# Soft mixture of experts after pooled attention, on one core: value scale from ScalarE's sums of magnitudes, the first batch's low value parts on GpSimd, and matmuls of ones in TensorE's empty stretches of the first blocks

## The chip, the core and the metric

The kernel runs on one core of one Trainium2 chip. The metric is the time of one execution in device microseconds. The engines are TensorE (PE in the profile; its weight loads are PEld), VectorE (DVE), ScalarE (ACT), GpSimd (POOL) and SyncE (SP, which issues DMAs). Each works through its own queue in order, and they meet by semaphores.

## What is computed

Keys and values are pooled 4 by 4, multiplied by a weight, and used both as keys and as values of attention; its output feeds a soft mixture of experts. Sizes: batch 4, 12288 queries per batch, 768 keys, 128 channels; 8 experts of 4 slots each.

```python
kv_pool = kv.reshape(B, H // r, r, W // r, r, C).mean(axis=(2, 4))
kv_flat = kv_pool.reshape(B, -1, C) @ w_sr
k = v = kv_flat
s = scale * (q @ k.transpose(0, 2, 1))
a = np.exp(s - s.max(-1, keepdims=True))
a /= a.sum(-1, keepdims=True) + 1e-09
x = (a @ v).reshape(B * N, C)
logits = x @ phi
d = np.exp(logits - logits.max(0, keepdims=True))
d /= d.sum(0, keepdims=True) + 1e-09
slot_input = (d.T @ x).reshape(E, S_per_e, D)
# each expert: relu(slot_input[e] @ w1[e]) @ w2[e] -> slot_out
c = np.exp(logits - logits.max(1, keepdims=True))
c /= c.sum(1, keepdims=True) + 1e-09
out = c @ slot_out
```

## The kernel before, in words

The queries are cut into 96 blocks of 512 (24 per batch). For a block TensorE computes scores of all 768 keys, in six tiles of 128 keys by 512 queries, two tiles to a PSUM buffer (`s0`, `s1`, `s2`). For accuracy q and k are split into a high and a low part, so a tile is three matmuls (lines 494 to 496), and a block 18. VectorE takes the row maximum: three transposing reductions (501) as the buffers fill, a reduction and a product with a mask (511, 513), one small matmul on TensorE (521), a reduction (526) and a transpose (531); then four subtractions (539), which also free the score buffers. ScalarE takes two exponentials of each half (546: the half-precision high part `phi`; 550: the full one), and GpSimd subtracts the two (555), which gives the low part `plo`. TensorE then multiplies these probabilities with the values, again in high and low parts (572, 573, 580). The next block's scores want the score buffers that the subtractions free.

Values stand beside their products with phi (`v`, 160 columns: 128 channels and 32 slots), and are scaled so that half-precision parts hold them. The scale is a power of two for each of the two column groups. `kv_m` takes the largest magnitude per partition on VectorE (399, joined in 404). `kv_d` spreads it on a diagonal on ScalarE (408), `kv_s_mm` multiplies it with a matrix of ones on TensorE (412), and `kv_s_g` takes the maximum over the row, cuts it to its exponent, and gives scale and inverse (419 to 425). `kv_t_hi` and `kv_t_lo` make the high and low half-precision parts `vhi` and `vlo`: for the first batch ScalarE scales and rounds in one step (445), and VectorE makes the low part (458); for the later batches ScalarE scales in place and rounds (442, 443), and GpSimd subtracts (454).

The first batch is loaded in pieces of key halves (512 and 256 keys) that VectorE adds up as they land (330, 332) to `pooled` (334). A matmul gives the half's keys (365), ScalarE rounds them to `khi` (369), VectorE makes `klo` (374), and 386 with 389 gives the values. Later batches are added up by DMA and take the same steps while the batch before them still computes.

The program's order is not written by hand. `Plan.op` takes each piece of work with its engine, a cost, what it depends on, a priority, a time `at` from which it may stand, and PSUM buffers that it takes (`acq`) or uses. `emit` walks through an imagined time and always takes the piece that can start first, among those within 0.12 us the lowest priority number; `hot` pieces are held to be urgent, and a piece with `fill` is taken, until the imagined time given, only where it ends before any other could start. What results is a fixed order per engine; at run time only semaphores decide when each starts.

Of the kernel before, what the change touches and what calls it, by code (L numbers as in the profile page):

```python
# [186 lines left out]
def attention_then_soft_moe(ctx: ExitStack, tc: tile.TileContext, qT, kv0, kvT, w_sr, w_srT, phi, w1, w2, outT):  # L187
# [203 lines left out]
    def kv_m(b, k, h):  # L391
        if k == 0 and h == 0:
            AM[b] = (
                bp.tile([P, 2, 2], F32, tag="am", name=f"am_{b}", bufs=1),
                bp.tile([P, 2, P], BF16, tag="dg", name=f"dg_{b}", bufs=1),
                bp.tile([P, 2], F32, tag="am2", name=f"am2_{b}", bufs=1),
            )
# [1 line left out]
        nc.vector.tensor_reduce(
            out=am[:, k, h : h + 1], in_=VU[b][:, 3 * h : 3 * h + 3, VSRC[k]], axis=XY, op=ALU.max,  # L400
            apply_absolute_value=True,
        )
# [12 lines left out]

    def kv_s_g(b):
        pa = PK_.pop(b)
        pg = pa[:, 2 * P : 2 * P + 2]
        nc.vector.tensor_reduce(out=pg, in_=pa[:, : 2 * P].rearrange("p (k n) -> p k n", k=2), axis=X, op=ALU.max)
# [10 lines left out]
    def kv_t_hi(b, k):  # L430
# [10 lines left out]
        if b:  # L441
            nc.scalar.activation(v[:, :, src], v[:, :, src], AF.Copy, scale=inv[:, k : k + 1])
            nc.scalar.activation(part, v[:, :, src], AF.Copy)
        else:
            nc.scalar.activation(part, v[:, :, src], AF.Copy, scale=inv[:, k : k + 1])
# [846 lines left out]
```

## Time and profile before

| | |
|---|---|
| time, median of 3 runs | 1093.59 us (1092.59 to 1095.2) |
| time of the profiled execution | 1093.54 us |
| its span, first to last instruction | 1091.8 us |
| mean granted clock of TensorE | 0.973 |
| busy: TensorE | 1026.5 us (94%), 10098 matmuls |
| busy: VectorE | 988.0 us (90%) |
| busy: GpSimd | 870.9 us (80%) |
| busy: ScalarE | 823.3 us (75%) |
| DMA | 89.15 MB, mean 82 GB/s |

A page of the profile gives busy shares over the span, groups of instructions with their mean time, and the chain of work that ended last. A row of the timeline reads: start, duration, engine, line, operation, output and inputs; in square brackets the idle time ahead of it and what ended it. Rows of TensorE overlap, since matmuls are pipelined and their ends are modelled: the start of one to the start of the next is what a matmul costs in a full stretch. A row of windows gives, for a stretch of time, the busy time of PE, PEld, DVE, ACT and POOL, then the granted clock of TensorE, the DMA share and GB/s.

### The profile page before, as it was taken

How to read it: one execution, taken by the hardware profiler on the slowest of the kernel's cores; microseconds unless marked ns; L12 is line 12 of the kernel's file. 1: busy time of each engine (PE TensorE's matmuls, PEld its weight loads, DVE VectorE, ACT ScalarE, POOL GpSimd, SP SyncE). 2: the span in 40 equal slices, each digit the busy share in tenths (PEclk: the TensorE clock that was granted, in tenths of full speed). 3: DMA queues.
4: the chain of work that ended last, by engine and by line, in shares of the span. 5: the costliest groups of instructions: out<-in, count | busy, mean ns of one | idle time of the engine just before them, and what ended most of it. 6: DMA issues, size and time to landing. Idle time of an engine off the chain costs nothing.

```text
span 1091.8 us, 24577 instructions
## 1 busy us (share of the span) xinstructions
PE 1026.5 (94%) x10098; PEld 883.1 (81%) x10098; DVE 988.0 (90%) x1583; ACT 823.3 (75%) x1029; POOL 870.9 (80%) x503
## 2 busy tenths in 40 slices
PE   3699999999999999999999999999999999997876
PEld 2488888888888888888888888988888888886443
DVE  7899999999899999999999999999999999997895
ACT  1677778779778878878878788788788777875564
POOL 0578998888989998889999988889888898883340
PEclk9699999999999999999999999999999999999885
DMA  9306501111126401120136310120110110113398
GB/s 344 124 12 148 123 16 40 41 59 40 40 43 143 97 16 40 40 64 35 40 69 146 83 40 1 40 98 2 40 40 2 40 41 2 40 40 118 143 413 368
DMA packets 17408, 89.15 MB, mean 82 GB/s; under 512 B 1680, under 2 KB 3984, under 8 KB 11152
## 3 DMA queue, kind: packets, MB, share of 16 engines
q1 hardware_dynamic: 13408, 69.47, 17.6%
q0 software_dynamic: 3312, 17.70, 8.5%
q8 instruction: 80, 1.31, 0.5%
q10 hardware_dynamic: 576, 0.41, 0.1%
q14 instruction: 32, 0.26, 0.1%
HBM read 58.87 MB, written 25.17 MB: 77 GB/s over the span
## 4 chain that ended last, share of the span: by engine, by line
PE 84%; DVE 7%; ACT 6%; issue 2%; DMA 0%; POOL 0%; SPq 0%; DVEq 0%; ACTq 0%
PE m L572 14%; PE m L580 14%; PE m L573 13%; PE s L494 12%; PE s L496 11%; PE s L495 11%; PE m L732 2%; ACT phi L546 2%; ACT t L550 2%; PE po L1177 2%; DVE o L1186 2%; PE m L521 1%; DVE pool L332 1%; DVE t L539 1%; DVE r L501 1%
## 5 line engine op out<-in xcount | busy, mean ns | idle before, releaser
L555 POOL TENSOR_TENSOR plo<-t,phi 128x1536 f16<-128x1536 f32 x190 | 596.0, 3143 | 116.2 <-ACT t L550 102.1
L546 ACT ACTIVATE phi<-t,lnk 128x1536 f16<-128x1536 f32 x192 | 301.1, 1570 | 141.7 <-DVE t L539 141.7
L501 DVE TRANSPOSE_TENSOR_REDUCE r<-s 128x32 f32<-128x1024 f32 x288 | 355.6, 1238 | 12.2 <-PE s L496 4.6
L572 PE MATMUL m<-vhi,phi 128*128 128x161 f16 x2280 | 356.3, 234 | 8.7 <-DVE m L526 5.4
L573 PE MATMUL m<-vlo,phi 128*128 128x160 f16 x2280 | 355.5, 233 | 0.0
L539 DVE TENSOR_TENSOR t<-s,mb 128x1024 f32<-128x1024 f32 (+1 forms) x384 | 341.1, 949 | 6.9
L550 ACT ACTIVATE t<-t,lnk 128x1536 f32<-128x1536 f32 x192 | 300.9, 1568 | 0.9
L494 PE MATMUL s<-qhi,khi 128*128 128x512 f32 x576 | 240.5, 418 | 6.6 <-DVE t L539 6.6
L572 PEld LDWEIGHTS <-phi 128*128 128x128 f16 x2304 | 223.9, 98 | 23.3 <-issue 23.3
L573 PEld LDWEIGHTS <-phi 128*128 128x128 f16 x2304 | 225.2, 98 | 10.8 <-issue 10.6
L496 PE MATMUL s<-qhi,klo 128*128 128x512 f32 x576 | 227.5, 395 | 0.0
L580 PE MATMUL m<-vhi,plo 128*128 128x161 f16 x2280 | 227.1, 234 | 0.0
L495 PE MATMUL s<-qlo,khi 128*128 128x512 f32 x576 | 226.9, 394 | 0.0
L580 PEld LDWEIGHTS <-plo 128*128 128x128 f16 x2304 | 173.0, 98 | 0.6 <-issue 0.6
L484 POOL TENSOR_TENSOR qlo<-q,qhi 128x512 fp32r<-128x512 f32 x96 | 126.5, 1318 | 27.1 <-ACT qhi L480 27.1
L494 PEld LDWEIGHTS s<-qhi,khi 128*128 128x128 f32 x576 | 109.8, 191 | 27.0 <-issue 4.0
L496 PEld LDWEIGHTS s<-qhi,klo 128*128 128x128 f32 x576 | 109.3, 190 | 24.6 <-DVE klo L374 0.4
L495 PEld LDWEIGHTS s<-qlo,khi 128*128 128x128 f32 x576 | 110.2, 191 | 19.7 <-issue 0.7
L590 ACT ACTIVATE xl<-m 128x322 f32<-128x322 f32 x189 | 80.9, 428 | 43.9 <-PE m L580 42.6
L531 DVE STREAM_TRANSPOSE mb<-m 128x512 f32<-128x512 f32 x96 | 68.3, 711 | 3.3
L480 ACT ACTIVATE qhi<-q 128x512 fp32r<-128x512 f32 x96 | 59.2, 618 | 2.2 <-issue 1.3
L526 DVE TENSOR_REDUCE m<-m 128x16 f32<-128x64 f32 x96 | 21.5, 224 | 36.5 <-PE m L521 36.5
(146 smaller groups left out, 836.8 us busy)
## 6 DMA issues: line engine op xcount, KB each, us to landing
q<-qT SPq DMA_DIRECT2D x23, 1024.0 KB, 5.0
outT<-o SPq DMA_DIRECT2D x21, 1024.0 KB, 5.8
kva<-kvT POOLq DMA_DIRECT2D x9, 1536.0 KB, 11.3
kva<-kvT SPq DMA_DIRECT2D x3, 1536.0 KB, 9.9
kv<-kv SPq DMA_DIRECT2D x8, 512.0 KB, 5.7
w<-w SPq DMA_DIRECT2D x2, 1536.0 KB, 7.6
w<-w SPq DMA_DIRECT2D x4, 768.0 KB, 4.2
outT<-o SPq DMA_DIRECT2D x6, 512.0 KB, 4.1
```

The costliest lines, as they stand in the source:

```text
L484: nc.gpsimd.tensor_tensor(out=lo, in0=q_src(i), in1=hi.bitcast(F32), op=ALU.subtract)
L494: nc.tensor.matmul(s, khi[:, ks], hi, start=True, stop=False)
L495: nc.tensor.matmul(s, khi[:, ks], lo, start=False, stop=False)
L496: nc.tensor.matmul(s, klo[:, ks], hi, start=False, stop=True)
L501: nc.vector.tensor_reduce(out=MX[i][:, 2 * u : 2 * u + 2, :].rearrange("p t b -> p (t b)"), in_=S[i, u].rearrange("p t (b j) -> p (t b) j" ...
L539: nc.vector.tensor_tensor(out=TT_[i, h][:, o : o + n, :], in0=S[i, t // 2][:, u : u + n, :], in1=MX[i].unsqueeze(1).broadcast_to([P, n, BQ ...
L546: nc.scalar.activation(hi, TT_[i, h], AF.Exp, bias=lnk, scale=SCALE)
L550: nc.scalar.activation(t, t, AF.Exp, bias=lnk, scale=SCALE)
L555: eng.tensor_tensor(out=lo, in0=TT_.pop((i, h)), in1=PP[i, h], op=ALU.subtract)
L572: nc.tensor.matmul(px, p, vhi[:, t, :], start=(t == 0), stop=False)
L573: nc.tensor.matmul(px[:, 1:], p, vlo[:, t, :], start=False, stop=False)
L580: nc.tensor.matmul(px, PP[i, t // TH][1][:, t % TH, ks], vhi[:, t, :], start=False, stop=(t == NT - 1))
```

## The change

There are three parts.

*Scale.* The row maxima on VectorE give way to sums of magnitudes: ScalarE's activation with the absolute value and an accumulator (`kv_a`, four per batch; its elementwise output `rest` is not used). A cast to bfloat16 (`kv_b`) and two matmuls with the ones give the sum over all partitions and both halves, which `kv_s_g` cuts to its exponent; the scale constant VK becomes 16384.

*First batch.* It now takes the path of the later ones: ScalarE scales in place and rounds, and GpSimd makes the low parts. Its value steps have other priorities, and its `klo` is marked urgent.

*Matmuls of ones.* 45 matmuls of the ones by themselves, 128 by 512 in bfloat16, whose output nothing reads: a first chain of 15 into the score buffer `s2`, and 30 into the two small PSUM buffers `m`, as `fill` pieces up to the plan's time of 47.

```diff
-VK = 4096.0
+VK = 16384.0
...
+    WARM = (("s2", 9.4, 15, 0.42), ("m", 27.5, 30, 0.22))
+    WDUE = 47.0
+    VBASE = 19.0
+    VSTEP = 1.5
...
-    def kv_m(b, k, h):
+    def kv_a(b, k, h):
...
-        nc.vector.tensor_reduce(
-            out=am[:, k, h : h + 1], in_=VU[b][:, 3 * h : 3 * h + 3, VSRC[k]], axis=XY, op=ALU.max,
-            apply_absolute_value=True,
-        )
-        if h and k:
-            nc.vector.tensor_reduce(out=am2, in_=am, axis=X, op=ALU.max)
-
-    def kv_d(b, k):
-        _, dg, am2 = AM[b]
-        nc.scalar.activation(dg[:, k, :], ident, AF.Copy, scale=am2[:, k : k + 1])
+        nc.scalar.activation(
+            rest, VU[b][:, 3 * h : 3 * h + 3, VSRC[k]], AF.Abs, scale=1.0 / VK, accum_out=AM[b][0][:, h, k : k + 1],
         )
+
+    def kv_b(b):
+        nc.scalar.activation(AM[b][1], AM[b][0], AF.Identity, bias=tiny)
 
     def kv_s_mm(b):
         pa = PK_[b] = mt([P, 512], f"pa_{b}")
-        nc.tensor.matmul(
-            pa[:, : 2 * P], ones, AM.pop(b)[1].rearrange("p k n -> p (k n)"), start=True, stop=True
-        )
+        ab = AM.pop(b)[1]
+        for h in range(2):
+            nc.tensor.matmul(pa[:, :2], ones, ab[:, h, :], start=(h == 0), stop=(h == 1))
 
     def kv_s_g(b):
-        pg = pa[:, 2 * P : 2 * P + 2]
-        nc.vector.tensor_reduce(out=pg, in_=pa[:, : 2 * P].rearrange("p (k n) -> p k n", k=2), axis=X, op=ALU.max)
-        nc.vector.tensor_scalar_max(pg, pg, 1e-30)
-        nc.vector.tensor_single_scalar(pg.bitcast(U32), pg.bitcast(U32), 0x7F800000, op=ALU.bitwise_and)
-        nc.vector.tensor_scalar_mul(g, pg, 1.0 / VK)
+        nc.vector.tensor_single_scalar(g.bitcast(U32), PK_.pop(b)[:, :2].bitcast(U32), 0x7F800000, op=ALU.bitwise_and)
...
+    def warm(n, ring):
+        t = mt([P, 512], f"wm_{n}") if ring == "m" else ps.tile([P, 2, BQ], F32, tag=ring, name=f"wm_{n}")[:, 0, :]
+        tv = t.rearrange("p (a b) -> p a b", b=P)
+        nc.tensor.matmul(tv, ones, ones.unsqueeze(1).broadcast_to([P, 4, P]), start=True, stop=True)
+
+    def warm_ops(name, ring, at, n, cost, prio, deps):
+        for k in range(n):
+            deps = [op("PE", cost, 0.1, prio, deps, lambda k=k: warm(f"{name}{k}", ring), acq=[(ring, ("wm", name, k))], at=at + k * cost, fill=WDUE)]
...
+    for j, (ring, at, n, cost) in enumerate(WARM):
+        warm_ops(j, ring, at, n, cost, 500.0, [ops["w"]])
```

TensorE at the start of the program, before: `pooled` is the first batch's added-up keys, `w_sb` the weight, `s_0` the first score buffer, and a row's brackets name the semaphores that it waits for.

```order
L826 MATMUL m_116<-phi_sb,wT_sb 128x32 [waits DMAHW3_49,DMAHW2_49]
L365 MATMUL m_117<-pooled_118,w_sb 128x512 [waits DMAHW0_49,DVE_49]
L386 MATMUL m_116<-w_sb,pooled_118 128x160 [waits Activation_49]
L386 MATMUL m_116<-w_sb,pooled_118 128x160 x2
L494 MATMUL s_0_176<-qhi_136,khi_162 128x512 [waits Activation_49]
```

The same place in the changed kernel (where 826 is line 811 and 365 is 371; `wm` is the output of the matmuls of ones).

```order
L811 MATMUL m_118<-phi_sb,wT_sb 128x32 [waits DMAHW3_49,DMAHW2_49]
L837 LDWEIGHTS ones [waits DVE_49]
L837 MATMUL wm_136<-ones 128x512
L837 LDWEIGHTS ones
L837 MATMUL wm_140<-ones 128x512 [waits PE_49]
...
L837 MATMUL wm_191<-ones 128x512 [waits PE_49]
L371 MATMUL m_119<-pooled_120,w_sb 128x512 [waits DMAHW0_49,DVE_49]
```

Fifteen matmuls of ones stand ahead of the first key matmul, and from the second on each waits for TensorE's own semaphore, that is, for the one before it to be through.

VectorE around the first `klo`, before, among the adds of the second key half:

```order
L330 TENSOR_TENSOR pool_161<-kv_139 128x512 [waits DMAHW5_49,DMAHW4_49]
L332 TENSOR_TENSOR pool_161<-pool_161,kv_148 128x512 [waits DMAHW6_49,DVE_49]
L332 TENSOR_TENSOR pool_161<-pool_161,kv_148 128x512 [waits DMAHW7_49,DVE_49]
L374 SCALAR_TENSOR_TENSOR klo_163<-m_117,khi_162 128x512 [waits Activation_49]
L332 TENSOR_TENSOR pool_161<-pool_161,kv_148 128x512 [waits DMAHW0_49,DVE_49]
```

And in the changed kernel:

```order
L336 TENSOR_TENSOR pool_193<-kv_147 128x512 [waits DMAHW5_49,DMAHW4_49]
L338 TENSOR_TENSOR pool_193<-pool_193,kv_170 128x512 [waits DMAHW6_49,DVE_49]
L380 SCALAR_TENSOR_TENSOR klo_195<-m_119,khi_194 128x512 [waits Activation_49]
L338 TENSOR_TENSOR pool_193<-pool_193,kv_170 128x512 [waits DMAHW7_49,DVE_49]
L338 TENSOR_TENSOR pool_193<-pool_193,kv_170 128x512 [waits DMAHW0_49,DVE_49]
```

`klo` has moved ahead of one add: five adds follow it instead of four.

VectorE from block 0's last row maximum to its first subtraction, before (`am` are the magnitudes, `rq` what the row-maximum matmul reads, `mb` the spread maximum, `g` and `inv` scale and inverse):

```order
L399 TENSOR_REDUCE am_194<-v_0_166 128x1
L404 TENSOR_REDUCE am_0_196<-am_194 128x2 [waits DVE_49]
L501 TENSOR_REDUCE r_0_203<-s_2_209 128x32 [waits PE_49]
L511 TENSOR_REDUCE m_117<-r_0_203 128x16 [waits DVE_49]
L513 TENSOR_TENSOR rq_224<-m_117,quad 128x64 [waits DVE_49]
L526 TENSOR_REDUCE m_0_234<-m_117 128x16 [waits PE_49]
L531 STREAM_TRANSPOSE mb_236<-m_0_234 128x512 [waits DVE_49]
L419 TENSOR_REDUCE m_116<-m_116 128x2
L420 TENSOR_SCALAR m_116<-m_116 128x2 [waits DVE_49]
L421 TENSOR_SCALAR m_116<-m_116 128x2 [waits DVE_49]
L423 TENSOR_SCALAR g_241<-m_116 128x2 [waits DVE_49]
L425 RECIPROCAL inv_243<-g_241 128x2 [waits DVE_49]
```

In the changed kernel, to the first subtraction:

```order
L486 TENSOR_REDUCE r_0_232<-s_2_242 128x32 [waits PE_49]
L496 TENSOR_REDUCE m_119<-r_0_232 128x16 [waits DVE_49,PE_49]
L498 TENSOR_TENSOR rq_263<-m_119,quad 128x64 [waits DVE_49]
L420 TENSOR_SCALAR g_265<-m_118 128x2 [waits Activation_49]
L422 RECIPROCAL inv_267<-g_265 128x2 [waits DVE_49]
L511 TENSOR_REDUCE m_0_273<-m_119 128x16 [waits PE_49]
L516 STREAM_TRANSPOSE mb_280<-m_0_273 128x512 [waits DVE_49]
L524 TENSOR_TENSOR t_0_287<-s_0_207,mb_280 128x1024 [waits DVE_49]
```

The maxima are gone, and scale and inverse have moved from behind the transpose to between the row-maximum matmul's input and its reader.

TensorE behind block 0's scores in the changed kernel (before, one matmul of the diagonals and the row-maximum matmul stood there, and then block 1): three matmuls of ones, the product of the sums, two of ones, and then

```order
L506 MATMUL m_119<-rq_263,sel_r 128x64 [waits DVE_49]
L837 LDWEIGHTS ones
L837 MATMUL m_118<-ones 128x512 [waits DVE_49]
L837 LDWEIGHTS ones
L837 MATMUL m_119<-ones 128x512 [waits DVE_49]
...
L837 MATMUL m_119<-ones 128x512
L479 MATMUL s_0_299<-qhi_269,khi_194 128x512 [waits DVE_49,PE_49,Activation_49]
```

Ten matmuls of ones stand between block 0's row-maximum matmul and block 1's scores; the first waits for `g` to be read, the second for VectorE's reading of the row maxima. Behind block 1's scores stand nine, its row-maximum matmul, and six more, the third of which waits for VectorE. GpSimd makes `vlo` of the first batch between the low parts of the second and the third block's queries.

More of the change, by code (lines that the diff above doesn't have):

```diff
@@ L440, in kv_t_hi @@
         part = hi[:, :, src.start + 1 : src.stop + 1]
[L441 to L445, printed above, removed]
+        nc.scalar.activation(v[:, :, src], v[:, :, src], AF.Copy, scale=inv[:, k : k + 1])
+        nc.scalar.activation(part, v[:, :, src], AF.Copy)
     def kv_t_lo(b, k):
@@ L857, in kv_ops @@
             at_["kh", h] = op("ACT", act(n), 0.1, p, [at_["k", h]], lambda h=h: kv_k_hi(b, h), use=[("m", ("pk", b, h))])
[L858 removed]
+            at_["kl", h] = op("DVE", dve(n), 0.08, p, [at_["kh", h]], lambda h=h: kv_k_lo(b, h), use=[("m", ("pk", b, h))], hot=not b)
             ops["k", b, h] = at_["kl", h]
[L860 removed]
+        vb, vs = (base, step) if b else (VBASE, VSTEP)
+        m = []
         for h in range(2):
[L862 to L864 removed]
+            p = vb + vs * (2 + h)
             at_["v", h] = op("PE", 0.85, 0.3, p, dep0[h] + dep1, lambda h=h: kv_v_mm(b, h), use=kvu, acq=[("m", ("pv", b, h))] + ([("v32", b)] if h == 0 else []))
@@ L867, in kv_ops @@
             for k in range(2):
-                m[k].append(op("DVE", (0.53 if k == 0 else 0.2) + 0.2 * h * k, 0.08, p + step * (1 + 0.4 * k), [at_["vo", h]] + m[k] + m[0][:1], lambda h=h, k=k: kv_m(b, k, h), use=[("v32", b)]))
-        d = [op("ACT", 0.4, 0.1, base + step * 5, m[0] + m[1], lambda k=k: kv_d(b, k)) for k in range(2)]
-        s = op("PE", 0.25, 0.4, base + step * 5.5, d, lambda: kv_s_mm(b), acq=[("m", ("pa", b))])
-        s = op("DVE", 1.1, 0.08, base + step * 5.5, [s], lambda: kv_s_g(b), use=[("m", ("pa", b))])
+                m.append(op("ACT", act(3 * (C if k == 0 else NS)) + 0.2, 0.1, p + vs * (1 + 0.4 * k), [at_["vo", h]] + m[-1:], lambda h=h, k=k: kv_a(b, k, h), use=[("v32", b)], raw=0.15))
+        d = op("ACT", 0.2, 0.1, vb + vs * 5, m, lambda: kv_b(b), raw=0.15)
+        s = op("PE", 0.1, 0.3, vb + vs * 5.5, [d], lambda: kv_s_mm(b), acq=[("m", ("pa", b))])
+        s = op("DVE", 0.36, 0.08, vb + vs * 5.5, [s], lambda: kv_s_g(b), use=[("m", ("pa", b))], fill=vb + vs * 5.5 + 14.0)
         prev = [s] + dep1
@@ L874, in kv_ops @@
             n = NT * (C if k == 0 else NS)
-            a = op("ACT", act(n, 1) * (2 if b else 1), 0.1, base + step * (6 + k), prev, lambda k=k: kv_t_hi(b, k), use=[("v32", b)])
-            ops["t", b, k] = op("POOL" if b else "DVE", 2.1 * n / 1000 + 0.3 if b else dve(n) + 0.06, 0.08, base + step * (6 + k), [a], lambda k=k: kv_t_lo(b, k), use=[("v32", b)])
+            a = op("ACT", act(n, 1) * 2, 0.1, vb + vs * (6 + k), prev, lambda k=k: kv_t_hi(b, k), use=[("v32", b)])
+            ops["t", b, k] = op("POOL", 2.1 * n / 1000 + 0.3, 0.08, vb + vs * (6 + k), [a], lambda k=k: kv_t_lo(b, k), use=[("v32", b)])
             prev = [a]
+    for j, (ring, at, n, cost) in enumerate(WARM):
+        warm_ops(j, ring, at, n, cost, 500.0, [ops["w"]])
     kv_ops(0, -60, 1.5, [[ops["pool", 0, R2 - 2], ops["wo"]], [ops["pool", 1, R2 - 2], ops["wo"]]], [])
```

25 lines of the change are left out of this document (7 added, 18 removed).

## The prediction

> **What bounds the kernel now.** I read the page's chain first, then the clock in windows, then the timeline of the first 60 us.
>
> ```profile
> PE 84%; DVE 7%; ACT 6%; issue 2%; DMA 0%; POOL 0%; SPq 0%; DVEq 0%; ACTq 0%
> ```
>
> TensorE carries 84% of the chain that ends last. Once it runs without holes, a block costs what its matmuls cost, and other engines' work is hidden. So I look for where it has holes.
>
> ```profile
> 0.00:52.00 52.00, 24.79 (x75) 18.35 (x75) 40.78 (x66) 18.58 (x21) 14.71 (x14) 0.84 0.66 245
> 52.00:230.00 178.00, 177.05 (x1757) 156.86 (x1757) 164.87 (x250) 139.70 (x164) 153.38 (x81) 1.00 0.26 61
> 230.00:300.00 70.00, 68.04 (x701) 60.25 (x700) 63.93 (x103) 57.51 (x73) 62.54 (x37) 1.00 0.13 47
> 470.00:530.00 60.00, 58.86 (x611) 52.08 (x611) 55.65 (x93) 49.21 (x62) 55.01 (x33) 1.00 0.12 44
> 710.00:770.00 60.00, 58.87 (x614) 51.91 (x612) 55.61 (x96) 49.23 (x63) 53.47 (x32) 1.00 0.13 45
> ```
>
> The first two numbers of a row are the stretch's length and TensorE's busy time. Up to 52 us it is busy for 24.8 of 52; from there it idles 0.95 us in 178. At the three changes of batch it idles 1.96, 1.14 and 1.13 us, 4.2 in all. So the change can win in the head, up to the first product of probabilities and values at 52.05, and at most some 4 us behind it. A shift of that first product reaches the end of the program.
>
> **The clock.** The column behind the five busy times is the granted clock; the windows have the length at which it changes in this trace.
>
> ```profile
> 26.20:29.61 3.41, 1.86 (x7) 0.77 (x5) 3.38 (x7) 1.59 (x4) 0.00 (x0) 1.00 0.98 418
> 29.61:33.02 3.41, 0.42 (x1) 0.29 (x1) 2.65 (x11) 0.76 (x3) 2.49 (x2) 0.50 0.92 384
> 33.02:36.44 3.42, 2.30 (x6) 1.84 (x6) 3.42 (x7) 1.75 (x3) 0.00 (x0) 0.50 0.01 4
> 36.44:39.85 3.41, 3.41 (x10) 2.60 (x9) 2.55 (x4) 3.38 (x3) 0.66 (x1) 0.50 0.00 0
> 39.85:43.26 3.41, 1.45 (x7) 0.89 (x5) 2.84 (x4) 2.73 (x3) 3.41 (x2) 1.00 0.00 0
> 43.26:46.68 3.42, 1.01 (x3) 0.81 (x4) 3.13 (x5) 0.43 (x2) 3.33 (x2) 0.50 0.63 187
> 1046.78:1050.20 3.42, 2.04 (x20) 1.16 (x19) 3.42 (x6) 3.13 (x6) 0.92 (x2) 1.00 1.00 414
> 1053.61:1057.02 3.41, 2.23 (x20) 1.35 (x24) 3.41 (x6) 2.08 (x5) 1.05 (x1) 1.00 1.02 416
> 1057.02:1060.44 3.42, 3.42 (x26) 1.93 (x22) 2.84 (x6) 1.97 (x4) 1.13 (x2) 0.50 1.00 412
> ```
>
> After a full window the clock rises (36.44, then 1.00). After one busy for 2.30 of 3.42, 67%, it does not. It falls after 1.86 and 1.45 of 3.41; in the tail 2.04 was enough to keep it and 2.23 once was not. So rising wants between 67% and all of a window, and falling has its border near 60%. Score blocks 1 and 2 (the second and third) thus start at half clock:
>
> ```profile
> 36.41 0.63 PE L496 MATMUL s<-qhi,klo 128*128 128x512 f32 x1
> 36.84 0.63 PE L494 MATMUL s<-qhi,khi 128*128 128x512 f32 x1
> ...
> 40.55 0.39 PE L495 MATMUL s<-qlo,khi 128*128 128x512 f32 x1
> 40.77 0.39 PE L496 MATMUL s<-qhi,klo 128*128 128x512 f32 x1
> 41.20 1.25 DVE L501 TRANSPOSE_TENSOR_REDUCE r<-s 128x32 f32<-128x1024 f32 x1 [0.31 <-PE s L496]
> ```
>
> A 512-column matmul follows the next after 0.43 us at half clock and 0.22 to 0.23 at full clock: a block of 18 takes 4.1 us at full clock. The last matmul streams until 41.00 and its reader starts at 41.20: 0.2 us to hand on.
>
> The Trainium skill, page "TensorE: Matmul & The Clock Gate", section "What's actually happening", has the clock fall after at least one idle window of about 3.4 us. The row of 26.20 differs: no window was idle and yet it fell at 29.61. By the page the fillings between the blocks would have nothing to hold and block 1 would run warm in both kernels; the sum below goes by the rows.
>
> **The head, step by step.**
>
> ```profile
> 8.59 0.60 PE L826 MATMUL m<-phi_sb,wT_sb 128*128 128x32 f32 x2 [8.59 <-DMA phi_sb<-phi]
> 17.79 2.08 PE L365 MATMUL m<-pooled,w_sb 128*128 128x512 f32 x2 [8.60 <-DVE pooled L334]
> 18.37 1.42 DVE L332 TENSOR_TENSOR pool<-pool,kv 128x512 f32<-128x512 f32 x2
> 20.53 0.69 DVE L374 SCALAR_TENSOR_TENSOR klo<-m,khi 128x512 fp32r<-128x512 f32 x1 [0.74 <-ACT khi L369]
> 24.04 0.42 DVE L334 TENSOR_TENSOR pooled<-pool 128x256 f32<-128x256 f32 x1
> 24.38 0.70 DVE L399 TENSOR_REDUCE am<-v 128x1 f32<-128x384 f32 x2
> 25.00 1.24 DVE L501 TRANSPOSE_TENSOR_REDUCE r<-s 128x32 f32<-128x1024 f32 x1
> ...
> 28.41 1.24 DVE L501 TRANSPOSE_TENSOR_REDUCE r<-s 128x32 f32<-128x1024 f32 x1
> 30.78 0.22 DVE L526 TENSOR_REDUCE m<-m 128x16 f32<-128x64 f32 x1 [0.51 <-PE m L521]
> 31.04 0.71 DVE L531 STREAM_TRANSPOSE mb<-m 128x512 f32<-128x512 f32 x1
> 31.67 0.40 DVE L419 TENSOR_REDUCE m<-m 128x2 f32<-128x256 f32 x1
> 32.79 1.20 DVE L539 TENSOR_TENSOR t<-s,mb 128x1024 f32<-128x1024 f32 x1
> 34.14 0.77 PE L494 MATMUL s<-qhi,khi 128*128 128x512 f32 x1 [3.40 <-DVE t L539]
> 35.21 2.41 DVE L539 TENSOR_TENSOR t<-s,mb 128x512 f32<-128x512 f32 x3
> 43.74 0.71 DVE L531 STREAM_TRANSPOSE mb<-m 128x512 f32<-128x512 f32 x1
> 44.48 3.55 DVE L539 TENSOR_TENSOR t<-s,mb 128x1024 f32<-128x1024 f32 x4
> 45.85 0.77 PE L494 MATMUL s<-qhi,khi 128*128 128x512 f32 x1 [2.41 <-DVE t L539]
> 52.05 0.24 PE L572 MATMUL m<-vhi,phi 128*128 128x161 f16 x1
> ```
>
> VectorE is never idle here for long: it sets block 0's end, and TensorE waits for it twice (3.40 and 2.41 us).
>
> *The first chain of fifteen.* It stands ahead of L365 on TensorE, and each link waits for the one before. No row shows such a self-wait; between 0.43 us (none) and 0.43 + 0.2 = 0.63 (as from TensorE to VectorE), I take 0.63, as the wait is the same kind of signal. That is a duty of 67%, the one that did not raise the clock. From 9.2 us, where L826 ends, the last link starts at 9.2 + 14 x 0.63 = 18.0 and L365 at 18.45: 0.7 us later than now, at half clock as now. klo follows at 21.2 (20.53 + 0.7). It now stands ahead of the second pooling add, so five adds follow instead of four, one more by 0.72: pooled ends 0.7 + 0.7 = **1.4 us later**, at 25.9. With links at 0.43 the delay is nothing, and a clock that is up by 17.8 gives 1.0 us on L365 (2.08 against some 1.0 at twice the clock).
>
> *Block 0 on VectorE.* The pair of maxima at 24.38 goes: the first row maximum, now at 25.00, starts at 25.9, +0.9. The second pair and its join, which stand ahead of the third (28.41), go too; but that one now waits for TensorE's second key half, whose steps hang on pooled, and I put it 0.5 later, at 28.9. Behind the transpose, five small steps (31.67 to 32.79, 1.12 us) go; the two that are left, some 0.45 us by their share, fit the 0.51 us in which VectorE waits for the row-maximum matmul ahead of 30.78. The transpose starts at 31.55, and subtraction follows 0.74 later as in block 1 (43.74, 44.48): 32.3 against 32.79, **-0.5**. Block 1's matmuls start at 33.65.
>
> *Block 1.* The subtractions run unbroken, 3.55 us as at 44.48, because the low parts, which stand in the hole between the first (to 33.99) and the others (from 35.21), go to GpSimd; they end at 35.9 instead of 37.6. Matmuls at full clock need 4.1 us, to 37.75, so VectorE's three maxima run on, 3 x 1.25, to 39.8. Now the third ends at 42.45. So block 2's matmuls start 2.65 us earlier, at 43.2: **-2.65**.
>
> *Block 2.* 45.85 to 52.05 is 6.2 us; at full clock 4.1: **-2.1**. The first product starts at 47.3: -4.75.
>
> *Covers.* GpSimd's low parts:
>
> ```profile
> L454 POOL TENSOR_TENSOR vlo<-v,vhi 128x768 f16<-128x768 f32 x3 | 4.8, 1597 | 0.0
> L389 ACT ACTIVATE v<-m 128x480 f32<-128x480 f32 x8 | 4.5, 559 | 1.4 <-PE m L386 1.4
> ```
>
> 1.6 us plus some 0.5 for the small part, from 33 to 35.3, before the first exponentials' low parts can start at 37.7; uncovered it would be 2.1. ScalarE gets four sums, each no dearer than the 0.56 us of 480 elements plus an unknown for the accumulator (0 to 0.3 us), ending near 29, while their result is read at 30.8: 1.8 us to spare. TensorE's product of the sums waits for them with block 0's row-maximum matmul queued behind it, which VectorE in turn waits for; that one is due at 30.8 as well, so a later sum would cost its lateness one for one. The fillings between the blocks are 0.22 us each: nine before block 1 (31.7 to 33.65) end just as its buffer comes free; nine behind it are over 0.6 us before the row maximum needs TensorE. If they ran at 0.43 they would be late by 1.9 us in each place.
>
> *Behind the head.* Per batch VectorE loses some 2.1 us (two pairs of maxima at 0.70 and 0.7 of small steps), ScalarE gains four sums and loses two diagonals. Bounds: all 4.2 us of holes gone, or 1.6 us more at each of three changes if the two large sums (some 0.5 + 0.3 each) come out where ScalarE has no slack, +4.8. I take **-0.5**: VectorE's small steps stand directly ahead of a row maximum there, but most holes have other causes.
>
> Sum: -4.75 - 0.5 = -5.25 against the profiled execution's 1093.54 us (span 1091.8 and 1.7 around it; the median of three is 1093.59, the same): **1088.3 us**.
>
> **Rivals.**
> A. The chain warms the clock by 17.8 or its links are shorter. For it: a full window raises the clock. Against: the window at 67% that did not. L365 1.0 earlier and no delay: 1.7 to 1.9 us less, 1086.5.
> C. The clock falls in the second gap, where six fillings and one row maximum leave a window near the border of 60%. Block 2 then runs as now: 2.1 us back, 1090.4. The Trainium skill, page "TensorE: Matmul & The Clock Gate", section "A second HAM failure mode: psum-queue depth-cycling", speaks against the change here: small idles between groups that cycle through PSUM banks let the clock swing. The tail's rows, 1.00 and 0.50 in turn, agree.
> D. ScalarE becomes the bound at the changes of batch: +4.8 in place of -0.5 eats the head's gain, 1093.6.
> E. Slower: the fillings do not hold the clock at all (the change does not do what it says). They still stand in order ahead of block 1, block 1's row maximum and block 2: nine at 0.43 push block 1 from 33.65 to 35.6, 1.5 later than now, at half clock; nine more push its row maximum to 3.3 later, and block 2 starts 3.4 later than now: 1097. It decides from the point where a gap's window falls below the border.
>
> **How the numbers follow.** Forecast 0.52, A 0.17, C 0.12, D 0.08, E 0.05; 0.06 for a larger gain behind the head (1086). The range 1085.6 to 1091.2 takes in A, C and 2 to 3 us of unknown behind the head, and leaves out D, E and a little. About 0.2%, 2.2 us, is what a measurement of this kernel can tell from no change: faster (below 1091.4) 0.87, same 0.08 (D), slower 0.05 (E).
>
> **What would show it.** The spacing of the chain's links, and where L365 starts (18.45 in the forecast, 17.8 in A); pooled's end near 25.9; granted clock 1.00 from block 0 to the end of block 2; block 1's first matmul near 33.65, block 2's near 43.2, first product near 47.3; the idle time at the three changes near 4 us still. I am wrong if that product starts where forecast and the end does not follow, or if the clock reads 0.50 in blocks 1 and 2.

## The result, and the profile after

| | before | after |
|---|---|---|
| time, median of 6 runs | 1093.55 us (1092.59 to 1095.37) | 1086.61 us (1085.88 to 1087.86) |
| ratio, 95% interval | | 0.9936 (0.9926 to 0.9945) |
| profiled execution, its span | 1093.54, 1091.8 us | 1086.81, 1085.0 us |
| mean granted clock | 0.973 | 0.984 |
| first product of probabilities and values | 52.05 us | 47.06 us |

The changed kernel is 0.64% faster. The two profiled executions differ by 6.73 us: 4.99 lie ahead of the first product, 1.74 behind it. TensorE still carries 83% of the chain that ends last. The windows of the changed kernel, for the same stretches as before (stretch, its length, busy PE, PEld, DVE, ACT, POOL, then clock, DMA share, GB/s):

```profile
0.00:52.00 52.00, 39.28 (x190) 23.39 (x191) 41.32 (x63) 23.57 (x33) 20.84 (x19) 1.00 0.65 245
52.00:230.00 178.00, 176.58 (x1746) 156.16 (x1744) 164.13 (x249) 142.28 (x175) 154.87 (x82) 1.00 0.28 67
230.00:300.00 70.00, 68.42 (x704) 60.71 (x702) 63.97 (x100) 57.67 (x73) 62.77 (x37) 1.00 0.09 32
470.00:530.00 60.00, 59.20 (x620) 52.62 (x618) 54.87 (x85) 50.00 (x64) 54.18 (x32) 1.00 0.11 36
710.00:770.00 60.00, 59.19 (x619) 52.59 (x617) 54.91 (x85) 50.09 (x63) 54.13 (x34) 1.00 0.11 36
```

The clock of the first row is 1.00 instead of 0.84. Neither number counts the start: the first clock record of the changed kernel lies at 22.09 us, and ahead of it the column reads 1.00 although nine matmuls fill the window from 18.68 to 22.09 and seventeen the one from 35.75 to 39.16, so that TensorE ran at half clock there, as before the change. At the three changes of batch TensorE idles 1.58, 0.80 and 0.81 us, 3.2 in all instead of 4.2. From 52 to 230 us it idles 1.42 instead of 0.95: something was given back there.

TensorE's timeline of the head, the stretch up to the first product (start, duration, engine, line, operation, count, idle ahead):

```profile
9.09 9.57 PE L837 MATMUL wm<-ones 128*128 128x512 bf16 x15
18.46 1.91 PE L371 MATMUL m<-pooled,w_sb 128*128 128x512 f32 x2
...
30.82 2.58 PE L837 MATMUL m<-ones 128*128 128x512 bf16 x10
37.56 2.12 PE L837 MATMUL m<-ones 128*128 128x512 bf16 x9
...
42.85 0.47 PE L479 MATMUL s<-qhi,khi 128*128 128x512 f32 x1 [1.08 <-DVE t L524]
...
47.06 0.24 PE L557 MATMUL m<-vhi,phi 128*128 128x161 f16 x1
```

The chain's fifteen links take 9.57 us, 0.64 each, and L371 starts at 18.46: where the forecast had it. And VectorE's:

```profile
21.64 3.59 DVE L338 TENSOR_TENSOR pool<-pool,kv 128x512 f32<-128x512 f32 x5
25.27 0.42 DVE L340 TENSOR_TENSOR pooled<-pool 128x256 f32<-128x256 f32 x1
...
32.02 3.55 DVE L524 TENSOR_TENSOR t<-s,mb 128x1024 f32<-128x1024 f32 x4
35.49 3.52 DVE L486 TRANSPOSE_TENSOR_REDUCE r<-s 128x32 f32<-128x1024 f32 x3
39.50 0.32 DVE L496 TENSOR_REDUCE m<-r 128x16 f32<-128x96 f32 x1 [0.50 <-PE m L837]
...
41.48 3.55 DVE L524 TENSOR_TENSOR t<-s,mb 128x1024 f32<-128x1024 f32 x4
```

Block 1's three maxima run on from the subtractions without a hole, since its scores come at full clock. New is the 0.50 us of idle ahead of the row maximum's second step (L496), put down by the profile to the nine matmuls of ones ("fillings" from here on) behind block 1's scores, which write the small bank that L496 writes too.

### The profile page after: what moved, and what is told of

It reads as the page before. It is cut to its first block, busy times and chain, and to the rows that moved or that the text cites. A ratio compares the mean times of both kernels' runs of the same rounds, so it can differ in the third digit from the quotient of the medians.

```text
span 1085.0 us, 24660 instructions
## 1 busy us (share of the span) xinstructions
PE 1030.9 (95%) x10147; PEld 881.0 (81%) x10147; DVE 979.3 (90%) x1549; ACT 827.3 (76%) x1059; POOL 873.4 (80%) x506
## 4 chain that ended last, share of the span: by engine, by line
PE 83%; DVE 7%; ACT 5%; issue 2%; DMA 1%; POOL 0%; SPq 0%; DVEq 0%; ACTq 0%
PE m L557 14%; PE m L565 14%; PE m L558 13%; PE s L479 12%; PE s L481 11%; PE s L480 11%; PE m L717 2%; DVE o L1181 2%; ACT phi L531 2%; ACT t L535 1%; PE m L506 1%; PE po L1172 1%; DVE pool L338 1%; DMA kv<-kv 1%; DVE t L524 1%
## 5 line engine op out<-in xcount | busy, mean ns | idle before, releaser
L479 PE MATMUL s<-qhi,khi 128*128 128x512 f32 x576 | 238.0, 413 | 1.1 <-DVE t L524 1.1
L469 POOL TENSOR_TENSOR qlo<-q,qhi 128x512 fp32r<-128x512 f32 x96 | 128.4, 1338 | 25.9 <-ACT qhi L465 25.9
L479 PEld LDWEIGHTS s<-qhi,khi 128*128 128x128 f32 x576 | 108.5, 188 | 21.3 <-issue 2.6
```

What stands on the lines that cost most here:

```text
L469: nc.gpsimd.tensor_tensor(out=lo, in0=q_src(i), in1=hi.bitcast(F32), op=ALU.subtract)
L479: nc.tensor.matmul(s, khi[:, ks], hi, start=True, stop=False)
```

## The experiments

Medians of 5 to 11 runs scatter by 1 us and more (the kernel before, run anew beside each round of experiments, gave 1093.03 to 1094.54), so what follows rests on the traces first. Two numbers are compared: the start of the first product, and how much earlier than before the row-maximum matmul of a block starts. The first block's number is 0, and batches change in blocks 21 to 24, 45 to 49 and 69 to 73 in this program's work. A trace is of one execution: for `nochain`, `onesonly`, `steps`, `nochain_cold` and `best` it was the longest that was timed, for `lowdve` and `chain_m` the shortest. The later columns can carry that with them, and block 95 alone shows no difference of a few tenths; the step from one block to the next is firmer.

| kernel | us, median (range) | ratio to before, 95% | first product | block 21 | 23 | 40 | 49 | 69 | 73 | 95 |
|---|---|---|---|---|---|---|---|---|---|---|
| changed | 1086.61 (1085.88 to 1087.86) | 0.9926 to 0.9945 | 47.06 | 4.53 | 5.56 | 5.32 | 6.16 | 6.08 | 6.88 | 6.84 |
| nochain | 1086.90 (1085.37 to 1087.40) | 0.9926 to 0.9951 | 46.77 | 4.87 | 5.90 | 6.01 | 6.80 | 6.84 | 7.60 | 7.65 |
| nofill | 1089.79 (1088.76 to 1090.83) | 0.9955 to 0.9980 | 51.08 | -0.14 | 0.89 | 1.00 | 1.81 | 1.70 | 2.45 | 2.53 |
| nones | 1089.64 (1088.43 to 1090.57) | 0.9956 to 0.9980 | 50.59 | 0.34 | 1.38 | 1.43 | 2.26 | 2.34 | 3.10 | 3.08 |
| onesonly | 1092.58 (1090.95 to 1094.25) | 0.9982 to 0.9999 | 51.81 | 0.14 | 0.10 | -0.46 | -0.48 | -0.52 | -0.52 | -0.60 |
| oldscale | 1089.80 (1088.70 to 1091.89) | 0.9961 to 0.9985 | 47.27 | 3.99 | 3.92 | 3.49 | 3.29 | 2.97 | 2.95 | 2.47 |
| steps | 1094.17 (1093.26 to 1095.20) | 0.9999 to 1.0017 | 46.63 | 4.65 | 4.00 | 2.75 | 1.51 | 1.07 | -0.10 | -0.28 |
| lowdve | 1087.63 (1085.75 to 1088.80) | 0.9932 to 0.9957 | 47.80 | 3.89 | 4.92 | 4.48 | 5.22 | 5.24 | 6.07 | 6.12 |
| chain_m | 1086.70 (1085.35 to 1087.93) | 0.9917 to 0.9945 | 45.80 | 5.30 | 6.33 | 6.00 | 6.81 | 6.76 | 7.55 | 7.47 |
| trim | 1086.61 (1085.93 to 1087.19) | 0.9916 to 0.9940 | 46.62 | 4.72 | 5.75 | 5.71 | 6.53 | 6.41 | 7.21 | 7.17 |
| nochain_cold | 1086.70 (1085.23 to 1087.49) | 0.9915 to 0.9940 | 46.82 | 4.82 | 5.85 | 5.78 | 6.56 | 6.46 | 7.21 | 7.14 |
| tailfill | 1085.90 (1084.78 to 1086.77) | 0.9910 to 0.9934 | 46.59 | 4.69 | 5.72 | 5.75 | 6.54 | 6.55 | 7.38 | 7.32 |
| best | 1086.28 (1085.53 to 1086.89) | 0.9923 to 0.9951 | 45.47 | 4.95 | 5.98 | 5.54 | 6.23 | 5.72 | 6.46 | 6.15 |

### The three parts, one by one

```diff
-    WARM = (("s2", 9.4, 15, 0.42), ("m", 27.5, 30, 0.22))
+    WARM = (("m", 27.5, 30, 0.22),)          # nochain
+    WARM = (("s2", 9.4, 15, 0.42),)          # nofill
+    WARM = ()                                # nones
```

The fourth, `onesonly`, is the kernel before with `warm`, `warm_ops` and the WARM of the change.

**nochain.** 

> The changed kernel without the first chain of fifteen matmuls of ones; the thirty fillings between the blocks stay. Theory (the chain only delays): the chain never fills a window and raises nothing, it holds TensorE until 18.1 us. Without it L371 starts near 17.75 us instead of 18.46, the clock rises at the end of the first window that the key matmuls and first scores fill, and the first product of probabilities and values starts 0.7 us earlier, near 46.4: 1085.9 us. Rival (the chain warms after all, by its share of the window that ends at 22.09): without it the clock rises one window (3.4 us) later, the first three score groups run at half clock, and the first product starts 1 to 2 us later than 47.06: 1087.6 to 1088.6 us.

L371 started at 18.02, behind a sum of pooling that in this execution began 0.31 us later than in the changed kernel (17.27 instead of 16.96): 0.75 us behind it instead of 1.50. The clock rose at 21.09, at the end of a window in which key matmuls and first scores kept TensorE busy for 3.07 of 3.41 us. The first product came at 46.77, 0.6 earlier if the 0.31 is taken off. So the chain delays by 0.6 to 0.75 us and warms nothing; the rival fell. The time shows no difference, though block 95 is 0.8 us earlier: the tail, from that block's row maximum to the end, took 109.9 us instead of 108.5.

**nofill.** 

> The changed kernel without the thirty fillings between blocks 0, 1 and 2; the chain stays. Theory (the fillings hold the clock): windows of about a third busy follow each of the two blocks, the clock reads 0.50 when block 1 and block 2 start, and each block is 1 to 2.1 us longer; the 0.50 us wait of block 1's row maximum on the fillings goes. First product at 48.5 to 50.7 us, 1088 to 1090.2 us. Rival (the clock falls only after a window with no work, as one page of the Trainium skill has it): the clock stays at 1.00, the 0.50 us wait goes, first product near 46.6, 1086.1 us.

Windows of this kernel, at the length in which its clock changes:

```profile
28.68:32.09 3.41, 0.48 (x3) 0.28 (x2) 3.05 (x8) 2.20 (x4) 1.33 (x2) 1.00 1.00 425
32.09:35.50 3.41, 2.37 (x6) 1.91 (x7) 3.22 (x4) 3.35 (x6) 2.93 (x3) 0.50 0.21 89
...
38.92:42.33 3.41, 1.44 (x7) 0.89 (x5) 2.77 (x4) 2.06 (x2) 2.38 (x2) 1.00 0.00 0
42.33:45.74 3.41, 0.99 (x3) 0.82 (x4) 3.19 (x5) 0.43 (x2) 3.10 (x1) 0.50 0.73 240
```

The clock fell after 0.48 and after 1.44 us of work, and neither window was empty. Both blocks started at half clock; the first product came at 51.08, 4.0 us later than with the fillings, 0.4 more than the theory's upper end. The 0.50 us of idle ahead of L496 was gone too, so the held clock may be worth some 0.5 more than that.

**nones.** 

> No matmul of ones at all: the sums of magnitudes on ScalarE and GpSimd's low parts alone. Theory (three parts add up): the clock falls between the blocks as before; the first product starts 47.06 - 0.7 (no chain) + 1.5 to 3.6 (clock) = 47.9 to 50 us against 52.05 before, and behind it the matmuls gain the same 1.9 us at the changes of batch as in the changed kernel: 1087.5 to 1089.6 us. Rival (what is gained behind the head comes with the fillings, by another alignment of the blocks): shift of the first product alone, 1.9 us more: 1089.4 to 1091.5 us.

The first product came at 50.59, 0.6 later than the theory's end, and the time fell to the edge of both ranges. The trace decides: behind the first product block 95 gains another 1.6 us (3.08 instead of 1.46), in the same three steps as the changed kernel. So they do not come with the fillings.

**onesonly.** 

> The kernel before with the matmuls of ones alone (chain and fillings); the scale is still from VectorE's maxima, the first low parts still on VectorE. Theory (the behind-head gain belongs to the scale): the clock stays up, block 2 is 2.1 us and block 1 up to 1 us shorter, the chain costs 0.7: first product near 49 to 50 us, and its shift against 52.05 is kept to the end within 0.4 us: 1090.5 to 1091.8 us. Rival (the behind-head gain comes with the head's alignment): 1.9 us less, 1088.6 to 1089.9 us, with the steps at the changes of batch to be seen.

Behind the first product nothing was gained; 0.8 us was lost in this execution, which at 1094.25 was the longest of eleven (median 1092.58), so that loss is not shown for the kernel. The head itself gained only 0.24, which neither theory had. In this order seventeen fillings stand between blocks 0 and 1, five within block 1's scores, eight between these and its row maximum, and none behind it:

```profile
40.50:43.92 3.42, 1.52 (x7) 0.56 (x5) 2.77 (x6) 2.41 (x3) 3.42 (x3) 1.00 0.00 0
43.92:47.33 3.41, 2.43 (x6) 1.99 (x7) 3.16 (x4) 1.92 (x2) 3.04 (x1) 0.50 0.70 231
```

Block 1 ran at full clock, block 2 again at half. From the start of one block's last score matmul to the next block's first, the two gaps were 6.7 us (27.81 to 34.49, clock held) and 5.3 us (39.59 to 44.90, clock lost); in the changed kernel they were 5.1 (28.25 to 33.39) and 5.5 (37.33 to 42.85), both held, the second with fifteen fillings. So the second gap's length did not lose the clock here; its fewer fillings are what is left, and the old scale with as many there was not run. The parts therefore do not add up alone: `nones` gains 1.46 us in the head and `onesonly` 0.24, together they gain 4.99. Taken in turn, the scale and the low parts give -1.46 (52.05 to 50.59), the chain +0.49 (to 51.08), the fillings -4.02 (to 47.06).

### What was gained at the changes of batch

```diff
 # oldscale: the old kv_m, kv_d, kv_o_mm (256 columns) and kv_o_g for b > 0, cut to one line
+        if b:
+            d = [op("ACT", 0.4, 0.1, base + step * 5, mo[0] + mo[1], lambda k=k: kv_d(b, k)) for k in range(2)]
 ...
 # steps: in kv_s_g
+        if b:
+            nc.vector.tensor_reduce(out=x, in_=ident.rearrange("p (k n) -> p k n", k=2), axis=X, op=ALU.max)
+            nc.vector.tensor_reduce(out=x, in_=ident.rearrange("p (k n) -> p k n", k=2), axis=X, op=ALU.max)
+            nc.vector.tensor_scalar_max(x, x, 1e-30)
+            nc.vector.tensor_scalar_max(x, x, 1e-30)
```

**oldscale.** 

> The changed kernel with the old scale (maxima, diagonals and the five small steps on VectorE and ScalarE, the product of 256 columns) at the three changes of batch alone; the first batch and the head stay as changed. Theory (the 1.9 us behind the head come from VectorE's work at the changes of batch): the first product stays near 47.1 us, the shift of the row-maximum matmuls, now -4.5 at block 21 and -6.8 at block 95, stays near -4.5 or falls to -4.2: 1088.5 to 1089.2 us. Rival (they come from another alignment of the blocks, set in the head): the steps at blocks 22, 46 and 70 stay, 1086.6 us.

**steps.** 

> The changed kernel with four small dummy steps on VectorE (some 0.9 us, nothing reads them) behind the two that are left at each of the three changes of batch: the small steps are back, the maxima stay away. Theory (the small steps directly ahead of a row maximum hold TensorE): the row-maximum matmul of blocks 22, 46 and 70 is late again by 0.5 us or more each, the shift at block 95 is -4.2 to -5.3: 1088.1 to 1089.2 us. Rival (the maxima, 1.9 us of VectorE in each batch, were what counted, the small steps lie beside TensorE's work): 1086.6 to 1087.1 us.

The row-maximum matmuls of blocks 21, 22 and 23 in TensorE's timeline, of before, changed, steps and oldscale:

```profile
242.98 0.28 PE L521 MATMUL m<-rq,sel_r 128*128 128x64 f32 x1
253.64 0.30 PE L521 MATMUL m<-rq,sel_r 128*128 128x64 f32 x1 [0.28 <-DVE rq L513]
263.98 0.30 PE L521 MATMUL m<-rq,sel_r 128*128 128x64 f32 x1
```

```profile
238.46 0.28 PE L506 MATMUL m<-rq,sel_r 128*128 128x64 f32 x1
248.57 0.28 PE L506 MATMUL m<-rq,sel_r 128*128 128x64 f32 x1
258.43 0.27 PE L506 MATMUL m<-rq,sel_r 128*128 128x64 f32 x1
```

```profile
238.33 0.28 PE L512 MATMUL m<-rq,sel_r 128*128 128x64 f32 x1
250.12 0.30 PE L512 MATMUL m<-rq,sel_r 128*128 128x64 f32 x1 [1.46 <-DVE rq L504]
259.99 0.27 PE L512 MATMUL m<-rq,sel_r 128*128 128x64 f32 x1 [0.15 <-DVE rq L504]
```

```profile
238.99 0.28 PE L543 MATMUL m<-rq,sel_r 128*128 128x64 f32 x1
249.66 0.30 PE L543 MATMUL m<-rq,sel_r 128*128 128x64 f32 x1 [0.28 <-DVE rq L535]
260.06 0.30 PE L543 MATMUL m<-rq,sel_r 128*128 128x64 f32 x1
```

From 21 to 22: 10.66 us before, 10.11 changed, 11.79 with the dummy steps, 10.67 with the old scale. With the old scale TensorE waits the same 0.28 us as before, and none of the three steps of the gain is left: block 49 stands at 3.29 and 73 at 2.95, below the 3.99 of block 21. That is the theory of `oldscale`; block 95 stands 1.7 us lower than it said (2.47 for 4.2), as the shift also shrinks evenly from block to block, which stayed unexplained, and the median is 0.6 us over its upper end. The rival fell. The step from 21 to 22 does not hang on one trace: it is 10.11 to 10.13 in all ten kernels with the new scale and no dummies, 10.65 to 10.67 in the three with the old.

`steps` overshot. VectorE's timeline ahead of that matmul, and GpSimd's:

```profile
247.87 0.24 DVE L423 TENSOR_SCALAR xs<-xs 128x2 f32<-128x2 f32 x1
248.14 1.19 DVE L424 TENSOR_SCALAR xs<-xs 128x2 f32<-128x2 f32 x1
```

```profile
248.03 1.27 POOL L475 TENSOR_TENSOR qlo<-q,qhi 128x512 fp32r<-128x512 f32 x1
```

Of two equal steps L423 takes 0.24 us and L424 1.19: it ends at 249.33, just as GpSimd's subtraction of 248.03 ends (249.30). Instead of 0.9 the dummies cost 2.0. TensorE has no slack left behind it: 11.79 - 10.11 = 1.68 us are lost in block 22, and as much in blocks 46 and 70 (1.69 and 1.67). So the small steps stand on the path. The next step, 22 to 23, is 10.34 us before, 10.40 with the old scale, 9.86 changed and 9.87 with dummies. The dummies bring back the small steps but not the maxima, so the 0.48 us there belong to what else the old scale has: the maxima, the diagonals and the product of 256 columns, which were not told apart.

### The low parts of the first batch

```diff
-        nc.gpsimd.tensor_tensor(out=lo[:, :, src], in0=v[:, :, src], in1=hi[:, :, src.start + 1 : src.stop + 1], op=ALU.subtract)
+        nc.vector.scalar_tensor_tensor(            # b == 0 alone
+            out=lo[:, :, src], in0=v[:, :, src], scalar=inv[:, k : k + 1], in1=hi[:, :, src.start + 1 : src.stop + 1],
+            op0=ALU.mult, op1=ALU.subtract,
+        )
```

**lowdve.** 

> The changed kernel with the first batch's low parts back on VectorE, in one step from the float values, between block 0's subtractions; the order then has 14 and 1 fillings around block 1's row maximum instead of 9 and 6. Theory (GpSimd's low parts take 1.2 us of VectorE off the path of block 1): block 1's last maxima end 1.2 us later, the 0.50 us wait on the fillings goes or stays with the longer row of them, the first product starts 0.7 to 1.2 us later than 47.06: 1087.3 to 1087.8 us; with the clock fallen in the second gap 2 us more, 1089.5 us. Rival (VectorE has slack there, block 1 is bound by TensorE): 1086.6 us.

First product 47.80, 0.74 later; median 1087.63, within the theory's range. The clock stayed at 1.00. VectorE's two low parts took 1.3 us (35.39 to 36.65), and the idle time ahead of the row maximum's second step was gone, as the theory allowed; so the 0.74 is about what is left of 1.3 after that 0.50.

### The chain, and the wait of the row maximum

```diff
-    WARM = (("s2", 9.4, 15, 0.42), ("m", 27.5, 30, 0.22))
+    WARM = (("m", 9.4, 24, 0.3), ("m", 27.5, 30, 0.22))                       # chain_m
+    WARM = (("m", 27.5, 15, 0.22), ("m", 37.5, 12, 0.3))                      # trim
+    WARM = (("m", 9.4, 24, 0.3), ("m", 27.5, 15, 0.22), ("m", 37.5, 12, 0.3)) # best
```

**chain_m.** 

> The changed kernel with the first chain in one of the two small banks instead of the score ring, 24 links instead of 15: all write one standing tile, so that no link waits for the one before. Theory (the self-wait is why the chain did not warm the clock): links follow each other after 0.43 us, a window is full by 16 us, the later links take 0.22 us, L371 runs at full clock (about 1.0 us instead of 1.91) and starts at 17.7 or before; the sum of pooling ends 0.5 to 1 us earlier than 25.69 and the first product starts near 46.2: 1085.8 us. Rival (a stream of ones does not raise the clock before the key matmuls, whatever its spacing): the chain runs to 19.4 us, L371 starts there and the first product is 1 us late, near 48: 1087.6 us.

```profile
9.03 7.81 PE L837 MATMUL m<-ones 128*128 128x512 bf16 x24
17.95 1.13 PE L371 MATMUL m<-pooled,w_sb 128*128 128x512 f32 x2 [1.12 <-DVE pooled L340]
```

24 links took 7.81 us; fifteen had taken 9.57. L371 took 1.13 us instead of 1.91. The clock rose at 14.00, behind a window that the links filled. The theory holds: the chain of fifteen did not warm because each link waited for the one before. (The number of links changed too, but the spacing is what the trace shows: the first full window holds nine of them, one of the slow chain seven at most.) The last sum of pooling started at 23.98 instead of 25.27, and the first product 1.26 us earlier. But block 7 has only 0.61 of it left (5.61 against 5.00): there TensorE waits 0.49 us for VectorE's row maximum, which it did not before. At block 95 it is 0.63, and the median is that of the changed kernel.

**trim.** 

> No chain, and 27 fillings instead of 30: the order has 5 ahead of block 1's row maximum and 7 behind it, instead of 9 and 6. Theory (the row maximum's 0.50 us wait is for the small bank that the nine fillings write, and lies on the path): five are done before VectorE's third maxima, the wait goes, the clock stays at 1.00 since the window keeps over 0.45 of streaming, and the first product starts 0.5 us earlier than the 46.77 of the kernel without the chain: 46.3; 1086.1 us and at most 1086.9. Rival (the nine are needed to hold the clock): it falls in the second gap, block 2 is 2 us longer, 1088.5 us.

Theory and rival both failed. The clock stayed, and the wait stayed too. VectorE's and TensorE's timelines of trim:

```profile
35.05 3.51 DVE L486 TRANSPOSE_TENSOR_REDUCE r<-s 128x32 f32<-128x1024 f32 x3
39.06 0.33 DVE L496 TENSOR_REDUCE m<-r 128x16 f32<-128x96 f32 x1 [0.50 <-DVE r L486]
```

```profile
37.12 1.25 PE L837 MATMUL m<-ones 128*128 128x512 bf16 x5
```

The five fillings end at 38.37, before the maxima (38.56), and 0.50 us of idle follow all the same, now put down to the maxima themselves. It was 0.50 to 0.52 in all eight kernels that have fillings and this sequence on VectorE, five fillings or nine. It was not there with three VectorE instructions more ahead of it (`lowdve`), nor in `nofill` and `nones`: there VectorE has the same instructions, but with no filling to wait for it lacks the separate semaphore instruction that stands ahead of L496 in the eight, and L496 follows the maxima at once (41.50 and 41.04).

**best.** 

> Put together what the runs found: the first chain of 24 in a small bank, fillings 5 and 7 around block 1's row maximum, 60 fillings behind the last block, and one more tiny VectorE instruction (a clearing of two columns that nothing reads) between the third maxima of block 1 and its row-maximum reduction, in place of which 0.50 us of waiting was seen with nine fillings and with five. Theory (that wait hangs on the place in VectorE's instruction stream, since it was there when the fillings had long ended and gone when three more instructions stood ahead): the reduction follows the clearing within 0.1 us, the first product starts near 45.4 us instead of 45.8, and the whole takes 1085.0 us. Rival (the wait belongs to the reduction's own semaphore on TensorE): 0.4 to 0.5 us idle stay ahead of the reduction, first product near 45.8, 1085.4 us. By either, no more than 1 us is to be had against the changed kernel, as VectorE takes back some of a shorter head in blocks 3 to 7; if the second gap's window falls under 0.45 of streaming, the clock falls and block 2 is 2 us longer.

```profile
37.74 0.06 DVE L494 MEMSET xs<- 128x2 f32 x1
37.90 0.33 DVE L498 TENSOR_REDUCE m<-r 128x16 f32<-128x96 f32 x1
```

One tiny instruction more, and the reduction follows it 0.10 us after its end. The rival fell: the separate semaphore instruction stands ahead of the reduction here too, at 37.8. So the idle time goes with the place in the instruction stream, as far as these kernels show. What happens there was not settled. One more sign: a packet of queue q14, which the page lists as instruction, moves with it. In the windows of the DMA queues it lies between 38 and 41 us in all eight kernels with the idle time, and between 32 and 34 in best, lowdve, nofill, nones and onesonly. In the eight it lands 0.6 to 0.9 us after L496 has started, so it is not what L496 waited for.

The shorter head did not reach the end. The first product is 1.6 us earlier than in the changed kernel, but block 95 is 0.7 later; some of it goes evenly over all blocks at equal idle time, which one execution cannot explain. Nor did the clock hold throughout: the chain ended 1.9 us before L371, the window from 15.91 to 19.32 held six matmuls (1.48 us), and the clock read 0.50 in the next, so the first scores ran at half clock again.

### Two more places

```diff
-            at_["kl", h] = op(..., use=[("m", ("pk", b, h))], hot=not b)
+            at_["kl", h] = op(..., use=[("m", ("pk", b, h))])          # nochain_cold, on nochain
+    d = [shi]                                                           # tailfill, on trim
+    for k in range(60):
+        d = [op("PE", 0.22, 0.1, T1 + 900, d, lambda k=k: warm(f"t{k}", "m"), acq=[("m", ("wm", "t", k))], fill=1e9)]
```

**nochain_cold.** 

> No chain, and the low part of the first keys again behind both pooling adds, as before the change. Theory (klo ahead of the second add leaves VectorE waiting 1.47 us instead of 0.75 and makes everything on it 0.7 us later): pooling ends 0.7 us earlier than in the kernel without the chain, the first product starts 0.4 to 0.7 us earlier, near 46.2: 1086.3 us. Rival (the first scores wait for klo, so that its place ahead of the add pays): the first maxima are late by as much as the add's 0.7 us, first product 46.8 to 47.5, 1087 us.

The rival's number: pooling ended 0.87 us earlier (24.12 instead of 24.99), and the third maxima started at 28.44, against 28.41. They wait for TensorE, 1.29 us instead of 0.20. Where klo stands makes no difference.

**tailfill.** 

> The kernel of the run before last (no chain, fillings 5 and 7) with 60 more fillings in the stretch behind the last block, where TensorE waits for ScalarE, VectorE and GpSimd a third of the time and the clock reads 0.50 in 7 of 22 windows of the changed kernel. Theory (fillings hold the clock there as between the first blocks, and half clock costs the end some 0.3 to 0.5 us per window): 0.50 in three windows or less from 1019 us on, 2 us less: 1084 us. Rival (the end is set by the evictions on ScalarE and VectorE; the fillings stand ahead of transposes and products): no change or up to 2 us slower, 1086 to 1088 us.

The windows behind the last block, of the changed kernel and of tailfill:

```profile
1019.00:1040.00 21.00, 14.36 (x136) 8.56 (x132) 20.24 (x35) 13.58 (x24) 9.16 (x9) 0.92 0.97 372
1040.00:1060.00 20.00, 15.92 (x119) 9.26 (x117) 19.27 (x35) 13.77 (x26) 8.83 (x10) 0.83 0.99 408
```

```profile
1019.00:1040.00 21.00, 19.60 (x160) 10.11 (x162) 20.90 (x35) 14.87 (x25) 9.27 (x9) 1.00 0.99 382
1040.00:1060.00 20.00, 18.90 (x146) 9.92 (x147) 18.36 (x34) 13.51 (x25) 9.49 (x10) 1.00 1.01 418
```

The clock was held, and nothing came of it: from block 95's row maximum to the end it is 108.3 us instead of 108.5. VectorE is busy there for 20.2 and 20.9 of 21 us, and the DMA engines almost throughout. The rival holds, though what sets the end, VectorE or the transfers, was not told apart. Its median, 1085.90, is the lowest of all, but its interval overlaps that of the changed kernel; no version was shown to beat it.

## Why the prediction was right, and where it was not

**The chain.** Links at 0.63 us measured 0.64, L371 at 18.45 came at 18.46, the end of pooling at 25.9 came at 25.69 (25.27 and 0.42). Its warming (rival A) fell: L371 took 1.91 us, and `chain_m` shows what a warm one takes, 1.13. That the total, 1086.81, is A's 1086.5 almost to the point is chance; by the time alone A would have been taken for the cause.

**Blocks 0 to 2.** First subtraction 32.02 against 32.3, block 2's scores 42.85 against 43.2, first product 47.06 against 47.3. The order of the terms is right: -0.77 at the first subtraction (forecast -0.5), -2.23 more by block 1 (-2.15), -1.99 more by block 2 (-2.1). Block 1's maxima ended earlier than worked out, at 39.0 instead of 39.8: the subtraction came 0.3 earlier, the three maxima took 3.52 together instead of 3.75, and the sum itself is 0.15 too high (35.9 and 3.75 make 39.65). The 0.50 us of idle ahead of L496, which the sum did not have, took more than half of that back. Where the prediction counts nine fillings ahead of block 1 there are ten; they ended as block 1 started (33.40 and 33.39).

**The clock.** It read 1.00 through both gaps, so C and E fell. The gaps' windows in the changed kernel:

```profile
28.92:32.33 3.41, 2.59 (x13) 0.98 (x12) 3.04 (x8) 2.19 (x5) 1.33 (x2) 1.00 0.99 418
39.16:42.57 3.41, 2.15 (x10) 0.66 (x8) 2.58 (x5) 1.37 (x1) 3.41 (x3) 1.00 0.05 10
```

2.15 of 3.41 us lies near the 60% that was taken for the border, and it kept the clock. That border was too high: 1.72 in `lowdve` and 1.85 in `trim` kept it as well (last section). `nofill` shows what the fillings are worth, 4.0 us of the head. The page "TensorE: Matmul & The Clock Gate" of the Trainium skill, section "What's actually happening", asks for an idle window before the clock falls; by it the fillings would have been worth nothing. Here it fell after windows with 1.44 and 1.52 us of work, so the measurement decides against it.

**Covers.** GpSimd's low parts were worth 0.74 us net (`lowdve`). ScalarE's large sums took 0.52 us and 0.19 for the accumulator, within the allowance of 0.3, and the last ended at 28.93, near the 29 of the forecast. The fillings between the blocks ended in time, as costed.

**Behind the head: the mis-sized term.** It was put at -0.5 with bounds of -4.2 and +4.8, and measured -1.74: -2.67 at the three changes of batch (block 21 to 23: 1.03; 40 to 49: 0.84; 69 to 73: 0.80; all differences of the table), and some 0.9 given back between them, of which 0.39 at block 8, where TensorE now waits 0.46 us for ScalarE's copy of a product, and did not before. VectorE's steps ahead of block 22's row maximum, before and changed:

```profile
251.91 0.40 DVE L419 TENSOR_REDUCE m<-m 128x2 f32<-128x256 f32 x1
...
253.02 0.31 DVE L511 TENSOR_REDUCE m<-r 128x16 f32<-128x96 f32 x1
```

```profile
247.38 0.12 DVE L420 TENSOR_SCALAR g<-m 128x2 uint32<-128x2 uint32 x1
247.53 0.17 DVE L422 RECIPROCAL inv<-g 128x2 f32<-128x2 f32 x1
247.62 0.31 DVE L496 TENSOR_REDUCE m<-r 128x16 f32<-128x96 f32 x1
```

The reason given, small steps directly ahead of a row maximum, is shown for 0.55, 0.54 and 0.54 us of the 2.67, the steps into blocks 22, 46 and 70: `oldscale` takes them away, and `steps` more than that. The other 1.04, 0.48 of it in the step into block 23, goes with the old scale too, but that 0.48 stays under the dummies, so it has one of the other causes named above. What went wrong was "but most holes have other causes": the size was judged by TensorE's holes, and a hole shows only part of the lateness, 0.28 of 0.55 us before and 1.46 of 1.68 in `steps`. VectorE's five steps there were 1.11 us (251.91 to 253.02), and the two left take 0.24. Rival D fell: the three changes of batch got shorter, not longer.
